# The last two token blocks: one finished and stored first, the other's products in two PSUM banks

## Chip, cores, metric

One core of a Trainium2 chip. The metric is device time in microseconds (us) of one execution; the profile's span, from the first to the last instruction, is about 1.8 us shorter than that time. Engines in the profile: PE is TensorE's matmuls, PEld its weight loads, DVE VectorE, ACT ScalarE, POOL GpSimd, SP SyncE; a q behind a name is that engine's sequencer. Li is line i of the kernel profiled.

## The reference

```python
qn = q / (norm(q, axis=1) + 1e-06);  kn = k / (norm(k, axis=1) + 1e-06)   # B, N, C = 4, 6144, 256
a  = softmax(kn.transpose(0, 2, 1) @ qn / tau)                            # C x C per batch
x  = (v @ a).reshape(B * N, C)                                            # 24576 tokens
h  = maximum(maximum(x @ w1, x @ w2), x @ w3)                             # d_ff = 768
return h @ w_out                                                          # 24576 x 256, float32
```

## The kernel before

The attention matrix is folded into the three weights of each batch, so a chunk of 512 tokens needs 36 products of 512 columns for `h` and 24 of 256 columns for `h @ w_out`. The last chunk is done in two halves of 256 tokens, so that less work is left when the last `h` is there. A token block is 128 tokens, `FC` = 6 pieces of `d_ff`, `P` = 128, `HT` = 2, `CC` = 2.

```python
ps_h = ...tile_pool(name="ps_h", bufs=6, space=PSUM)      # htile: one bank each
ps_x = ...tile_pool(name="ps_x", bufs=2, space=PSUM)      # xtile
...
def last_chunk(gi, aw, pending):
    ...
    def products(ps, t0, i, fcs):
        c0 = i * d_model if t0 == 0 else 0
        for fc in fcs:
            PE.matmul(ps[:, c0:c0 + d_model], lhsT=hts[gi][:, fc, (t0 + i) * P:(t0 + i + 1) * P],
                      rhs=wo_sb[:, fc, :], start=(fc == 0 and c0 == 0), stop=(fc == FC - 1), ...)
    ...                                   # first_half(i): blocks 0 and 1, one copy, one 256 KB store (L440)
    for fc in range(FC):
        h_block(gi, aw, fc, slice(HT, TPC), two_copies=fc in (0, 2, 3))
        if fc >= FC - HT:
            first_half(fc - (FC - HT))
    pss = [htile("o_ps") for _ in range(HT)]
    for fcs in (range(FC - 1), (FC - 1,)):            # the last piece of h is used last
        for i in range(HT):
            products(pss[i], HT, i, fcs)
    ACT.activation(out=o_sb[:, HT, :], in_=pss[0][:, 0:d_model], func=AF.Copy)       # L455
    DVE.tensor_copy(out=o_sb[:, HT + 1, :], in_=pss[1][:, 0:d_model])                # L456
    ACT.dma_start(out=dst[:, HT, :], in_=o_sb[:, HT, :])                             # L457
    SP.dma_start(out=dst[:, HT + 1, :], in_=o_sb[:, HT + 1, :])                      # L458
```

## Time and profile before

| | before |
|---|---|
| device time, median of the first 3 runs | 573.09 us (573.09 to 573.32) |
| span of the profile | 571.7 us |
| last product ends / last store issued | 568.09 / 568.58 |
| last store lands | 570.8 |

TensorE is busy for 97% of the span, and from 560 us on the chain is TensorE's without a gap, so what happens beside it there does not show in the time until it ends. The last 3.65 us, from there to the end, are a chain of a wait, a copy, a store and the closing of the program, and this is the stretch that the change is about. The lines that carry this are in the prediction below. Starts and ends are of the span's clock, so an event of one profile can be set against the same event of another only by its distance from a common point; for the end of this kernel that point is the end of TensorE's last product.

### The profile page before, as it was taken

How to read it: one execution, taken by the hardware profiler on the slowest of the kernel's cores; microseconds unless marked ns; L12 is line 12 of the kernel's file. 1: busy time of each engine (PE TensorE's matmuls, PEld its weight loads, DVE VectorE, ACT ScalarE, POOL GpSimd, SP SyncE). 2: the span in 40 equal slices, each digit the busy share in tenths (PEclk: the TensorE clock that was granted, in tenths of full speed). 3: DMA queues.
4: the chain of work that ended last, by engine and by line, in shares of the span. 5: the costliest groups of instructions: out<-in, count | busy, mean ns of one | idle time of the engine just before them, and what ended most of it. 6: DMA issues, size and time to landing. Idle time of an engine off the chain costs nothing.

```text
span 571.7 us, 9440 instructions
## 1 busy us (share of the span) xinstructions
PE 553.0 (97%) x3343; PEld 329.8 (58%) x3344; DVE 415.7 (73%) x658; ACT 310.4 (54%) x543; POOL 233.6 (41%) x237
## 2 busy tenths in 40 slices
PE   3789999999999999999999999999999999999997
PEld 2665555555755555555575555555575555555566
DVE  0048777777887778777768777777868778778775
ACT  1044567767464576776545467767645444444444
POOL 2441357776460078776560048777750000000000
PEclk9999999999999999999999999999999999999999
DMA  9996999884669268975279339984437333132112
GB/s 142 104 169 101 130 234 144 157 134 104 114 81 177 66 106 160 132 148 111 57 129 151 97 81 141 150 139 94 129 76 164 74 75 111 56 98 69 56 55 76
DMA packets 76960, 65.64 MB, mean 115 GB/s; under 512 B 52464, under 2 KB 62576, under 8 KB 76784
## 3 DMA queue, kind: packets, MB, share of 16 engines
q0 software_dynamic: 19072, 26.48, 38.8%
q1 hardware_dynamic: 57696, 38.41, 24.6%
q8 instruction: 26, 0.43, 0.3%
q14 instruction: 22, 0.18, 0.1%
q10 hardware_dynamic: 144, 0.13, 0.1%
HBM read 78.64 MB, written 25.17 MB: 182 GB/s over the span
## 4 chain that ended last, share of the span: by engine, by line
PE 93%; DMA 5%; POOL 0%; issue 0%; DVE 0%; POOLq 0%
PE h_ps L379 65%; PE o_ps L403 22%; DMA q_sb<-in_q_dram 5%; PE gram L250 3%; PE ew_ps L301 3%; POOL k_sb L99 0%; PE o_ps L428 0%; PE ew_ps L325 0%; PE warm_ps L464 0%; PE vt_ps L362 0%; PE gram L181 0%; DVE o_sb L456 0%; PE rs_ps L289 0%; PE gram L183 0%; PE rs_ps L319 0%
## 5 line engine op out<-in xcount | busy, mean ns | idle before, releaser
L379 PE MATMUL h_ps<-vt_sb,aw_sb 128*128 128x512 bf16 (+1 forms) x1764 | 406.7, 375 | 0.0
L379 PEld LDWEIGHTS <-aw_sb 128*128 128x128 bf16 x1764 | 171.7, 98 | 161.5 <-DVE aw_sb L307 2.5
L384 DVE TENSOR_TENSOR s_mx<-h_ps,s_mx 128x512 bf16<-128x512 f32 (+1 forms) x294 | 199.0, 677 | 81.8 <-ACT s_mx L383 81.5
L383 ACT ACTIVATE s_mx<-h_ps 128x512 bf16<-128x512 f32 (+1 forms) x294 | 172.6, 587 | 122.5 <-PE h_ps L379 121.4
L389 DVE TENSOR_TENSOR ht_sb<-h_ps,s_mx 128x512 bf16<-128x512 f32 (+1 forms) x291 | 199.0, 684 | 30.3
L209 POOL TENSOR_TENSOR acc<-acc,sq 128x768 f32<-128x768 f32 x88 | 144.3, 1650 | 69.3 <-ACT sq L201 53.2
L403 PE MATMUL o_ps<-wo_sb,ht_sb 128*128 128x256 bf16 x1128 | 153.8, 273 | 0.0
L403 PEld LDWEIGHTS <-ht_sb 128*128 128x128 bf16 x1128 | 110.4, 98 | 52.1
L406 ACT ACTIVATE o_sb<-o_ps 128x512 f32<-128x512 f32 x94 | 56.2, 598 | 83.6 <-PE o_ps L403 83.6
L110 POOL DMA_DIRECT2D v_sb<-in_v_dram x48 | 27.8, 583 | 37.3 <-DMA vt_sb<-v_sb 35.0
L201 ACT ACTIVATE sq<-q_sb 128x768 bf16<-128x768 fp8e4 x48 | 40.6, 846 | 0.0
L201 ACT ACTIVATE sq<-k_sb 128x768 bf16<-128x768 fp8e4 x48 | 40.1, 836 | 0.0
L206 POOL CAST acc<-sq 128x768 f32<-128x768 bf16 x6 | 4.9, 822 | 64.9 <-ACT sq L201 64.9
L102 POOL DMA_DIRECT2D q_sb<-in_q_dram x33 | 18.3, 562 | 4.1 <-DMA v_sb<-in_v_dram 3.5
L169 PE MATMUL kk<-k_sb 128*128 128x256 fp8e4 x48 | 7.5, 338 | 12.4 <-DVE k_sb L155 6.3
L99 POOL DMA_DIRECT2D k_sb<-in_k_dram x29 | 16.0, 553 | 3.2 <-DMA v_sb<-in_v_dram 1.3
L250 PE MATMUL gram<-k_sb,q_sb 128*128 128x512 fp8e4 x144 | 16.8, 277 | 0.0
L304 ACT ACTIVATE aw_sb<-ew_ps,rinv 128x384 bf16<-128x384 f32 (+1 forms) x24 | 13.2, 556 | 5.7 <-PE ew_ps L301 4.8
L250 PEld LDWEIGHTS <-q_sb 128*128 128x256 fp8e4 x144 | 15.9, 136 | 0.6
L222 POOL PARTITION_ALL_REDUCE tot<-acc x6 | 10.9, 1859 | 12.1 <-DVE s_mx L384 6.2
L301 PE MATMUL ew_ps<-w_sb,et 128*128 128x384 bf16 (+1 forms) x96 | 15.6, 313 | 0.0
L169 PEld LDWEIGHTS <-k_sb 128*128 128x256 fp8e4 x48 | 6.4, 182 | 13.3 <-DMA k_sb<-in_k_dram 7.1
(66 smaller groups left out, 120.5 us busy)
## 6 DMA issues: line engine op xcount, KB each, us to landing
out_dram<-o_sb SPq DMA_DIRECT2D x41, 512.0 KB, 2.9
v_sb<-in_v_dram POOLq DMA_DIRECT2D x48, 256.0 KB, 4.1
k_sb<-in_k_dram POOLq DMA_DIRECT2D x24, 192.0 KB, 5.7
q_sb<-in_q_dram POOLq DMA_DIRECT2D x24, 192.0 KB, 7.3
out_dram<-o_sb SPq DMA_DIRECT2D x13, 256.0 KB, 2.0
k_sb<-in_k_dram POOLq DMA_DIRECT2D x5, 256.0 KB, 11.2
w_sb<-in_moe_w_dram POOLq DMA_DIRECT2D x9, 128.0 KB, 5.6
kf<-in_k_dram SPq DMA_DIRECT2D x1, 1024.0 KB, 4.8
```

What stands on the lines that cost most here:

```text
L102: POOL.dma_start(out=qk[b][0][:, g0:g0 + w, :], in_=q_r[b][:, g0:g0 + w, :])
L110: POOL.dma_start(out=t, in_=v_r[gi // NCH, gi % NCH])
L201: ACT.activation(out=sq, in_=src, func=AF.Square)
L209: POOL.tensor_tensor(out=acc, in0=acc, in1=sq, op=ALU.add)
L250: PE.matmul(g[:, j * C:(j + 1) * C], lhsT=qt[:, tsl, j * P:(j + 1) * P], rhs=kt[:, tsl, :], start=(tp == 0 and j == 0), stop=(tp == NG // ...
L301: PE.matmul(ew[:, :w], lhsT=et[:, j, ic * P:(ic + 1) * P], rhs=w_sb[m][:, j, fsl], start=(j == 0), stop=(j == CC - 1))
L379: PE.matmul(t.rearrange("p (t n) -> p t n", n=P), lhsT=aw[m][:, ic, fsl], rhs=vt[:, tsl, ic, :], start=(ic == 0), stop=(ic == CC - 1))
L383: ACT.activation(out=s_mx, in_=hp[0], func=AF.Copy)
L384: DVE.tensor_tensor(out=s_mx, in0=hp[1], in1=s_mx, op=ALU.max)
L389: DVE.tensor_tensor(out=ht, in0=last, in1=s_mx, op=ALU.max)
L403: PE.matmul(st["ps"][:, half], lhsT=ht[:, fc, t * P:(t + 1) * P], rhs=wo_sb[:, fc, :], start=(fc == 0), stop=(fc == FC - 1))
L406: ACT.activation(out=st["o"][:, t - 1:t + 1, :].rearrange("p t d -> p (t d)"), in_=st["ps"], func=AF.Copy)
```

## The change

Intent: finish block 2 some products before block 3, so that its copy and store run while TensorE still works, and make the last step short: block 3's 256 columns are accumulated as two halves in two banks, ScalarE and VectorE each copy a half at the same time, and one store takes both. (Blocks are counted 0 to 3 in the last chunk; `block_1` in the code is block 3. The last store also moves from SP to ACT.)

```diff
--- before.py
+++ after.py
@@ -448,14 +448,26 @@
             h_block(gi, aw, fc, slice(HT, TPC), two_copies=fc in (0, 2, 3))
             if fc >= FC - HT:
                 first_half(fc - (FC - HT))
-        pss = [htile("o_ps") for _ in range(HT)]
-        for fcs in (range(FC - 1), (FC - 1,)):
-            for i in range(HT):
-                products(pss[i], HT, i, fcs)
-        ACT.activation(out=o_sb[:, HT, :], in_=pss[0][:, 0:d_model], func=AF.Copy)
-        DVE.tensor_copy(out=o_sb[:, HT + 1, :], in_=pss[1][:, 0:d_model])
-        ACT.dma_start(out=dst[:, HT, :], in_=o_sb[:, HT, :])
-        SP.dma_start(out=dst[:, HT + 1, :], in_=o_sb[:, HT + 1, :])
+
+
+        pa = htile("o_ps")
+        pb = [htile("o_ps") for _ in range(CC)]
+
+        def block_1(fcs):
+            for fc in fcs:
+                for d in range(CC):
+                    PE.matmul(pb[d][:, 0:P], lhsT=hts[gi][:, fc, (HT + 1) * P:(HT + 2) * P],
+                              rhs=wo_sb[:, fc, d * P:(d + 1) * P], start=(fc == 0), stop=(fc == FC - 1))
+
+        products(pa, HT, 0, range(FC - 1))
+        block_1(range(3))
+        products(pa, HT, 0, (FC - 1,))
+        block_1(range(3, FC))
+        DVE.tensor_copy(out=o_sb[:, HT, :], in_=pa[:, 0:d_model])
+        SP.dma_start(out=dst[:, HT, :], in_=o_sb[:, HT, :])
+        ACT.activation(out=o_sb[:, HT + 1, 0:P], in_=pb[0][:, 0:P], func=AF.Copy)
+        DVE.tensor_copy(out=o_sb[:, HT + 1, P:2 * P], in_=pb[1][:, 0:P])
+        ACT.dma_start(out=dst[:, HT + 1, :], in_=o_sb[:, HT + 1, :])
 
 
     ps = gram(0)
```

## The prediction

> **What bounds the kernel now.** I read the page first for the bound of the whole, then the chain that ended last, in order of time, for the final 12 us, then the timeline of the last microsecond of compute, then the sources of the final stores, and last the DMA view of the stretch in which nothing computes any more. The page:
>
> ```profile
> PE 553.0 (97%) x3343; PEld 329.8 (58%) x3344; DVE 415.7 (73%) x658; ACT 310.4 (54%) x543; POOL 233.6 (41%) x237
> ```
>
> TensorE is busy 97% of a span of 571.7 us, at full granted clock in all slices. The change touches nothing before the last 12 matmuls, so only the end matters. The chain, from 560 us on:
>
> ```profile
> 560.67 4.14 PE h_ps L379 x36
> 564.81 0.66 PE o_ps L428 x6
> 565.47 0.66 PE h_ps L379 x6
> 566.12 1.98 PE o_ps L428 x18
> 568.10 0.02 issue
> 568.13 0.42 DVE o_sb L456
> ```
>
> (start, length, what.) TensorE carries the chain without a gap until 568.10; then a copy of 0.42 us; then the view ends, though the span goes on to 571.7. Those 18 products are 6 of the first half's second block and the 12 that the change rearranges; 1.98 us over 18 is 0.110 us each. The timeline of the end:
>
> ```profile
> 566.92 0.42 DVE L389 TENSOR_TENSOR ht_sb<-h_ps,s_mx 128x256 bf16<-128x256 f32 x1
> ...
> 567.49 0.33 SPq L440 DMA_DIRECT2D out_dram<-o_sb  x1
> 568.02 0.39 ACT L455 ACTIVATE o_sb<-o_ps 128x256 f32<-128x256 f32 x1 [0.55 <-PE o_ps L428]
> 568.13 0.42 DVE L456 COPY o_sb<-o_ps 128x256 f32<-128x256 f32 x1 [0.78 <-PE o_ps L428]
> 568.43 0.41 ACTq L457 DMA_DIRECT2D out_dram<-o_sb  x1
> 568.58 0.33 SPq L458 DMA_DIRECT2D out_dram<-o_sb  x1
> ```
>
> The last ht is ready at 567.34; the two blocks' accumulations end one matmul apart (copies start at 568.02 and 568.13), so both 128 KB stores are issued nearly together, at 568.43 and 568.58. Their times to landing, each from its source line's view (first L457 on ACT's queue, then L458 on SP's):
>
> ```profile
> DMA to landing us min/median/max: 1.9/1.9/1.9
> DMA to landing us min/median/max: 2.2/2.2/2.2
> ```
>
> The landings are thus at 568.43 + 1.9 = 570.3 and 568.58 + 2.2 = 570.8, and the end is 0.9 us after the later one. The DMA view of 569.2 to 571.8 (40 slices of 0.065 us) says why the later issue takes longer:
>
> ```profile
> DMA  0048999999998500004000000000000000000000
> ...
> q1 hardware_dynamic: 144, 0.13, 14.5%
> q10 hardware_dynamic: 144, 0.13, 14.4%
> ```
>
> Both stores' data, 0.13 MB each, move in one unbroken stretch from slice 2 to slice 14, 569.33 to about 570.2. Looking at the same stretch in shorter windows, from 569.65 on all 144 packets of q1 (SP) are there but only 41 of q10 (ACT): ACT's data goes first and SP's starts when it is nearly through. One store alone needs about 0.4 us of that stretch, so SP's store waits some 0.25 to 0.3 us on the other. That is where 2.2 against 1.9 us comes from. The bound of the end is therefore: TensorE to 568.1, copy 0.42, issue, data queued behind the other block's data, landing, 0.9 us of closing.
>
> **What the Trainium skill says.** "TensorE: Matmul & The Clock Gate", section "Back-to-back issue gap", gives about 81 ns for each pair of weight load and matmul at N=128 in a sustained stream, and 134 cycles (56 ns at 2.4 GHz) for the isolated gap. This matters because 6 products of 256 columns become 12 of 128. The trace of before has eight N=128 bf16 products, each with its own weight load; in the chain near 36 us they read
>
> ```profile
> 35.86 0.45 PE vt_ps L362 x8
> ```
>
> which is 56 ns each. They are transposes, so the match isn't perfect, but the trace sides with 56 and I use it. "VectorE: DVE Perf Modes", section "The TRN2 errata — SBUF-src ops pay a fixed extra latency per instruction", gives PSUM to SBUF 120 + FD cycles for VectorE and 172 + FD for ScalarE, so halving a copy doesn't halve its time. The slopes in the trace agree: ScalarE 382 ns at 256 columns and 596 at 512 (0.836 ns a column), VectorE 418 to 425 and 688 (1.03 ns a column). "DMA: Bandwidth & Descriptors", section "Issuing engines are not separate DMA queues", says that transfers issued by different engines run on the same 16 DMA engines and interleave; the packets above agree that they share, though here one went almost wholly ahead of the other. "PSUM — Partial Sum Buffer", section "PSUM bank collisions raise a hardware error", is why the halves need two banks: ScalarE and VectorE may not read one bank at once. No run so far shows that.
>
> **The change part by part.**
>
> *TensorE.* Removed: 6 products of N=256 for the last block, 6 x 0.110 = 0.66 us. Added: 12 of N=128, 12 x 0.056 = 0.67 us. The sum is zero within 0.02 us; there are 6 more weight loads, which should hide. The order is new. The 12 products of before start at 568.10 - 12 x 0.110 = 566.78 in the chain's modelled ends. Now: pa's first five to 567.33; six halves to 567.67; pa's last to 567.78; six halves to 568.11. pa's last product needs the ht of 567.34 and is ready to issue only a third of a microsecond after that by ends, about 0.1 us when counted from its weight load, so no wait. The third PSUM buffer rotates onto one that VectorE's combination before the last read, finished about 566.5, while its first matmul is due after 567.1: no wait either.
>
> *The completed block ahead.* pa is complete at 567.78, so VectorE copies it 567.81 to 568.23 (0.425 us, gap of 0.03 as before) and SP issues its store at about 568.26, which is 0.17 us ahead of the first final issue of before. All of it lies beside TensorE's last halves.
>
> *The last block.* ScalarE copies 128 columns from 568.09 (its half ends one matmul earlier) in 386 - 128 x 0.836 = 279 ns, to 568.37. VectorE could start at 568.15, with a length of 425 - 128 x 1.03 = 292 ns. Its previous copy ends at 568.23; adjacent VectorE instructions in the trace start up to 0.08 us before the profiled end of the one before (566.06 + 0.42 against 566.40), so it starts between 568.15 and 568.23 and ends between 568.44 and 568.52. ACT issues about 0.03 later, at 568.47 to 568.55, in place of 568.58: a gain of 0.03 to 0.11, middle 0.07 us.
>
> *The landing.* SP's pa store starts its data about 0.8 to 0.9 us after issue (as ACT's did: 568.43 to 569.33), so 569.1 to about 569.45. The last store's data is due at 568.5 + 0.9 = 569.4, when the other is all but done. Its landing should take 1.9 to 1.95 us, in place of 2.24 (568.58 to 570.82, with the closing chain's semaphore wait): a gain of about 0.30 us.
>
> Sum: TensorE 0.00 (+0.02), issue -0.07, landing -0.30: about -0.36 us. Predicted time 573.09 - 0.36 = 572.73 us.
>
> **Rivals.** (a) The N=128 products cost the skill's 81 ns: 12 x 25 = 0.30 us more on TensorE, of which all moves the last copies. Time about 573.03. For: twice as many weight loads with half the stream to hide them, each 98 ns in the trace. Against: the 56 ns of the eight transposes, and four N=1 products in 0.08 us of the chain. (b) VectorE becomes the bound: its pa copy holds up the last half, and the store now waits for two engines. Worth 0.08 us at worst as computed, 0.1 more if the cross-engine wait is slow: 572.8 to 572.9. (c) The two stores' data still overlap, for they are only 0.2 to 0.3 us apart and each takes 0.35: then the landing stays at 2.1 to 2.2 and the time is 572.9 to 573.0. For: SP's 256 KB store of 567.49 is also still moving until about 569.0, just before pa's data. Against: it ends by then, and before, the same 256 KB had no visible effect. (d) More than thought: if the last store finds idle DMA engines and both copies overlap fully, 572.6. Nothing gets near 2% (11.5 us): from TensorE's end to the end of the span there are only 3.6 us.
>
> **Range and chances.** The runs of before spread over 0.23 us, as large as the effect. Rivals (a) to (c) each have perhaps one chance in six and all push towards 573.0; 572.45 at the low side allows for (d) and the spread, 573.10 at the high side for a gain lost entirely. Faster or slower by 2% would need a failure that this place in the program can't make.
>
> **What would show it.** After: the first combination-free product group should still begin near 566.1 and TensorE end within 0.05 us of 568.1 (later by 0.3: rival a). VectorE's 256-column copy should start near 567.8, before TensorE's end. The two short copies should be about 0.28 and 0.29 us and start within 0.15 us of each other. ACT's store should be issued at 568.5 and land in 1.9 to 2.0 us; if issue is earlier but landing 2.2, it was (c). The closing 0.9 us after the last landing should not change. The prediction is wrong if the last landing isn't 0.25 to 0.45 us before the old 570.8, or if TensorE waits inside the rearranged products.

## The result, and the profile after

| | before | after |
|---|---|---|
| device time, median of 6 runs | 573.11 us (573.01 to 573.97) | 572.90 us (572.74 to 573.17) |
| span of the profile | 571.741 | 571.391 |
| last product ends | 568.087 | 567.931 |
| last store issued | 568.578 | 568.347 |
| SP's wait for its landing ends | 570.822 | 570.473 |

The ratio is 0.9994, with a 95% interval of 0.9981 to 1.0007: no change that these runs can tell from none, and in the predicted range. (A ratio is the mean time of one kernel's fast runs over that of the other's of the same rounds, so it is not quite the ratio of the medians.) What the change may have done is therefore read from the two profiles, one of each kernel, and from nothing else.

The chain that ended last, in the kernel after, from 560 us on (start, length, what):

```profile
560.50 4.14 PE h_ps L379 x36
564.64 0.66 PE o_ps L428 x6
565.30 0.66 PE h_ps L379 x6
565.95 1.20 PE o_ps L428 x11
567.15 0.34 PE o_ps L459 x6
567.49 0.12 PE o_ps L428
567.61 0.02 issue
567.63 0.42 DVE o_sb L466
568.06 0.20 DVE o_sb L469
```

The whole line-up is 0.17 us earlier than before (560.50 against 560.67, with the same 4.14 us). The rest of the view is the changed end: six half products (L459) take 0.34 us, 56 ns each, and block 2's last product (L428) comes between the halves, without a gap. The chain leaves TensorE at 567.61 and goes through VectorE: its 256-column copy of block 2, then its half of block 3. The other six halves, which end at 567.93, are beside that copy. The view puts VectorE's second copy down to its first; but that copy starts 0.045 us after the halves end, so it is TensorE's end that it had to wait for (see rival (b) below).

The 0.17 us are not the change's. The same view of both kernels near 34 us, first before, then after:

```profile
34.00 0.32 PE gram L181
...
37.90 0.33 PE h_ps L379
```

```profile
33.88 0.31 PE gram L181
...
37.74 0.33 PE h_ps L379
```

The first batch's Gram products, which wait for q as it is loaded, are 0.12 us earlier in the profile of after, and the first `h` product 0.16 us. Both kernels run the same instructions there. Of the 0.350 us between the two spans, 0.17 were there before the changed part began; 0.18 are left for it.

The timeline of the end, after:

```profile
567.63 0.42 DVE L466 COPY o_sb<-o_ps 128x256 f32<-128x256 f32 x1 [0.46 <-PE o_ps L428]
567.91 0.28 ACT L468 ACTIVATE o_sb<-o_ps 128x128 f32<-128x128 f32 x1 [0.62 <-PE o_ps L459]
567.98 0.28 DVE L469 COPY o_sb<-o_ps 128x128 f32<-128x128 f32 x1
568.09 0.33 SPq L467 DMA_DIRECT2D out_dram<-o_sb  x1
568.35 0.37 ACTq L470 DMA_DIRECT2D out_dram<-o_sb  x1
```

VectorE copies block 2 before TensorE is done, its half of block 3 starts 0.06 us behind ScalarE's, and SP issues block 2's store (L467) 0.26 us ahead of the last one (L470). VectorE's half starts at 567.98, though its previous copy is shown to last until 568.06: the two overlap by 0.08 us.

The times from issue to landing, by source line, after: block 2's store (L467) in the first fence, the last one (L470) in the second, the 256 KB store of the first half (L440, the same line in both kernels) in the third:

```profile
DMA to landing us min/median/max: 1.9/1.9/1.9
```

```profile
DMA to landing us min/median/max: 2.1/2.1/2.1
```

```profile
DMA to landing us min/median/max: 2.0/2.0/2.0
```

The last store gained 0.1 us against the 2.2 of before, not 0.3. It takes longer than a store of twice the size. The DMA view of 568.8 to 571.4 in the kernel after, again 40 slices of 0.065 us:

```profile
DMA  3059999999999516000000000000000000000000
...
q1 hardware_dynamic: 161, 0.14, 15.9%
q10 hardware_dynamic: 144, 0.13, 14.5%
q14 instruction: 1, 0.01, 1.5%
```

The two stores' data still follow one another without a pause. Packet by packet, the trace has block 2's data (q1) from 568.94 to 569.44 and the last store's (q10) from 569.30 to 569.78: an overlap of 0.14 us. Before, the overlap was 0.14 us too (569.69 to 569.83); what differs is how long the second store had waited by then: its first packet came 1.11 us behind its issue, and now 0.95. In both kernels that packet starts 0.006 us after the first of the sixteen 4-byte packets that end the first store's data (569.682 and 569.688 before, 569.290 and 569.296 after). So the second store seems to take its turn behind the first still, with far less to wait.

From the end of the last product on, the end divides as follows (us; the times of packets and waits are of the trace's records, and each term is a difference of two of them; the fourth, from the last packet to the landing, is called the receipt below):

| | before (store on SP) | after (store on ACT) | gain |
|---|---|---|---|
| last product's end to last issue | 0.491 | 0.416 | 0.075 |
| issue to the store's first data packet | 1.110 | 0.949 | 0.161 |
| first data packet to the end of the last packet | 0.493 | 0.494 | 0.00 |
| last packet to the end of SP's wait for the landing | 0.641 | 0.683 | -0.04 |
| from there to the end of the span | 0.919 | 0.918 | 0.00 |
| sum | 3.654 | 3.460 | 0.194 |

TensorE gives 0.015 of this back (0.171 earlier at the start of the last stretch, 0.156 earlier at its end), which leaves 0.18.

The second row mixes two things. SP's stores that weren't held up began their data 0.83 to 0.86 us after issue, ACT's of before 0.914. An estimate from these (ACT's 0.914 is a single store): SP's last store had waited some 0.25 to 0.28 us behind the other one, ACT's waits 0.035 at most, and some 0.06 to 0.08 of the difference is given back because ACT starts later than SP. No run has the last store of the new order on SP.

### The profile page after: what moved, and what is told of

Its sections match the earlier page's. It is cut to its first block, busy times and chain, and to the rows that moved or that the text cites. A ratio compares the mean times of both kernels' runs of the same rounds, so it can differ in the third digit from the quotient of the medians.

```text
span 571.4 us, 9454 instructions
## 1 busy us (share of the span) xinstructions
PE 552.0 (97%) x3349; PEld 328.5 (57%) x3350; DVE 415.9 (73%) x659; ACT 310.0 (54%) x543; POOL 233.3 (41%) x237
## 4 chain that ended last, share of the span: by engine, by line
PE 94%; DMA 2%; issue 2%; POOL 1%; DVE 0%; POOLq 0%
PE h_ps L379 65%; PE o_ps L403 22%; PE gram L250 3%; PE ew_ps L301 3%; DMA q_sb<-in_q_dram 2%; POOL q_sb L102 0%; POOL k_sb L99 0%; PE o_ps L428 0%; PE gram L181 0%; PE ew_ps L325 0%; PE warm_ps L476 0%; PE gram L183 0%; PE vt_ps L362 0%; DVE o_sb L466 0%; PE o_ps L459 0%
## 5 line engine op out<-in xcount | busy, mean ns | idle before, releaser
L384 DVE TENSOR_TENSOR s_mx<-h_ps,s_mx 128x512 bf16<-128x512 f32 (+1 forms) x294 | 198.9, 677 | 82.2 <-ACT s_mx L383 81.9
L389 DVE TENSOR_TENSOR ht_sb<-h_ps,s_mx 128x512 bf16<-128x512 f32 (+1 forms) x291 | 199.0, 684 | 30.3
```

Of the source, the lines that this page charges most:

```text
L384: DVE.tensor_tensor(out=s_mx, in0=hp[1], in1=s_mx, op=ALU.max)
L389: DVE.tensor_tensor(out=ht, in0=last, in1=s_mx, op=ALU.max)
```

## The experiments

None gave a result, so nothing here is shown by experiment. Four kernels were made first, the changed one again and three that are each one step away from it.

**again**: the changed kernel, unaltered, to see how much of its end repeats.

> The changed kernel unaltered, to see what of its tail repeats. In its first profile the last product ended at 567.93, the last store was issued at 568.35 (0.42 later) and took 2.13 to land, against 2.24 before and 1.96 hoped for; its last data packet left at 569.79, so the receipt took 0.68 us, where the stores that were not last took 0.53 to 0.57. If the slow receipt is chance, this profile shows 1.95 to 2.0 from issue to landing; if it belongs to the kernel, 2.1 to 2.15 again. Last product's end to last issue should be 0.40 to 0.43 in either case. Time: 572.8 to 573.0, ratio 0.9994 to 0.9998 with an interval that includes 1.

(Its "0.53 to 0.57" for stores that were not last fits the first of each 128 KB pair alone; the 256 KB stores had 0.34 to 0.41.)

**order_only**: block 2 is still ahead, but block 3 is whole.

```diff
-        pb = [htile("o_ps") for _ in range(CC)]
+        pb = htile("o_ps")
-                for d in range(CC):
-                    PE.matmul(pb[d][:, 0:P], ...)    # cut short here
+                products(pb, HT, 1, (fc,))
-        ACT.activation(out=o_sb[:, HT + 1, 0:P], in_=pb[0][:, 0:P], func=AF.Copy)
-        DVE.tensor_copy(out=o_sb[:, HT + 1, P:2 * P], in_=pb[1][:, 0:P])
+        ACT.activation(out=o_sb[:, HT + 1, :], in_=pb[:, 0:d_model], func=AF.Copy)
```

> The first block still completed and stored ahead, but the last block's products whole (256 columns, one bank) and copied by ScalarE alone. Theory (the gain is the earlier first store, which takes its data out of the last store's way): last product's end to last issue 0.45 (0.04 wait, 0.386 copy, 0.03), so 0.03 later than with halves, issue to landing as in the changed kernel, 2.0 to 2.15, and the time within 0.1 us of the changed kernel's. Rival (the halved copies in two banks bring the gain): the time goes back to the 573.1 of before.

**halves_only**: the halves in two banks, but block 2 finished late.

```diff
-        block_1(range(3))
+        block_1(range(FC - 1))
         products(pa, HT, 0, (FC - 1,))
-        block_1(range(3, FC))
+        block_1((FC - 1,))
```

> The last block in halves of two banks, copied by both engines for one store, but the first block's last product only just before the last block's last two, as in the kernel before. Theory (the gain is the store ahead): VectorE's 256-column copy of the first block starts about 0.1 before TensorE's end and holds up its half copy, last product's end to last issue 0.55 to 0.65 in place of 0.42, the first store only 0.2 to 0.25 ahead, so issue to landing 2.1 to 2.25; end of last product to last landing 2.75 to 2.85, as before (2.73) or worse, time 573.0 to 573.2. Rival (the halves bring the gain): last issue 0.42 after the end as in the changed kernel, time 572.9.

**no_pa_store**: without block 2's store, a wrong result on purpose. REFUSED.

```diff
-        SP.dma_start(out=dst[:, HT, :], in_=o_sb[:, HT, :])
```

> Wrong result on purpose: the changed kernel without the store of the completed block, so that the last store has the DMA engines to itself. If the first store's data or receipts delay the last one, issue to landing falls from 2.13 to 1.9 to 1.98 and the time by 0.15 to 0.2 us below the changed kernel's. If the last store's receipt is slow whatever lies next to it, issue to landing stays at 2.05 to 2.1 (0.04 less for the data that starts unhindered).

Last, at 13:36, came one kernel that was to replay nine forms of the end side by side, each four times, so that the terms of the table above would have had repeats. No chip ran it either.

**replays**: no result.

```diff
+    for _ in range(4):
+        for tail in (tail_before, tail_after, tail_order, tail_halves, tail_alone, tail_nolead, tail_joint,
+                     tail_onsp, tail_small):
+            tail()        # 30 filler products, the first half's blocks, copy and store, then the form
+    # each tail writes to its own slice of a scratch tensor, so that no store waits for another's landing
```

> Nine forms of the end replayed in one kernel, four times each in turn, behind filler products, into scratch memory (ordinary fp8 Gram products in place of paired ones; its time, 850 to 950 us, says nothing). Read: P, end of last product to last issue; L, issue to landing. So far: before P 0.49, L 2.23; changed P 0.42, L 2.11. Theory: the gain is the store ahead. Rival: the halved copies bring it. Also: is the slow last receipt chance, a neighbour's doing, or a thing of the program's end. BEFORE 0.49, 2.2 to 2.25. AFTER 0.40 to 0.43; L 1.95 to 2.0 if the slow receipt is chance or the program's end, 2.1 if the neighbour's. ORDER (store ahead, last block whole in one bank, ScalarE's copy): P 0.45, L as AFTER; by the rival its sum is BEFORE's. HALVES (halves, first block completed only just before the end): P 0.55 to 0.65, L 2.1 to 2.25, sum no better than BEFORE; by the rival AFTER's sum. ALONE (AFTER without the first block's store): L 1.9 to 1.95, 0.05 below AFTER if only data overlaps, 0.15 to 0.2 if receipts suffer. NOLEAD (AFTER without the 256 KB store): as AFTER within 0.05. JOINT (one 256 KB store of both blocks at the end): L 2.1 to 2.25. ONSP (AFTER, last store issued by SP): L 0.05 to 0.1 shorter. SMALL (first block and left half of the last in one store ahead, the 64 KB right half last): P 0.35, L 0.1 to 0.2 shorter. Repeats should agree within 0.1 in L; where they spread more than forms differ, nothing is told apart.

So the questions in these texts stand open: which part of the change brought the 0.18 us, whether the slow last landing repeats, and what makes it slow.

## Why the prediction was right, and where it was not

The time, 572.90, was forecast as 572.73 within 572.45 to 573.10: inside the range and the class; the forecast was 0.17 too low. That says little: the range also holds the 573.09 of before, so no gain at all would have been inside it. By its steps:

- **TensorE unchanged** (forecast +0.02): 0.015 later. The twelve half products ran at 56 ns with a weight load each, as the eight transposes of before had said. Rival (a), the 81 ns that the Trainium skill's "TensorE: Matmul & The Clock Gate", section "Back-to-back issue gap", gives for a sustained stream, didn't come about in these two runs of six: it would have put TensorE's end 0.30 later.
- **No wait for `h` or for a bank**: right. The chain shows no gap inside the products. Block 2's last weight load started at 567.27; the `h` piece that it needs was done at 566.75 + 0.425 = 567.175, so 0.1 us was to spare.
- **Copies** (forecast 279 ns on ScalarE and 292 on VectorE, VectorE's start 0 to 0.08 behind): measured 277 and 284, VectorE's start 0.06 behind ScalarE's. Rival (b), VectorE's earlier copy in the way, came to nothing: its half started 0.045 after TensorE's end, about the 0.039 that the same copy took to start before. Scaling by the slope of measured sizes was right within 3% (VectorE's 1.03 ns a column mixes L389 at 256 columns with L384 at 512; like for like it is 1.04 to 1.05, and the forecast 290 to 292); a proportional guess (half of 386 and 425) would have been 0.07 to 0.08 us too short.
- **Last issue** (forecast 0.03 to 0.11 earlier, middle 0.07): 0.075.
- **Landing** (forecast 0.30 shorter, "1.9 to 1.95 us, in place of 2.24"): 2.126, so 0.118 shorter. This is the term that was mis-sized, and it is nearly all of the difference between the forecast 0.36 and the 0.18 found. The mechanism, that the second store's data waited on the first's, was there: its data started 0.161 sooner after issue. But I took the whole 1.96 us of before's first store as what a store takes once it is not held up, and that store differed from the one it stood for in two ways. It began its data 0.914 after issue, and the last store now took 0.949, which is 0.035. And its last packet was 0.552 ahead of the wait's end, where for the last store it was 0.683, which is 0.131. Together with 0.004 of data they make 0.170, the distance from 1.956 to 2.126; the rest of the shortfall of 0.18 is that I rounded 2.244 - 1.956 = 0.288 up to 0.30.

Rival (c), data that still overlap, has the right numbers (a landing of 2.1 to 2.2, 572.9 to 573.0 us), for the wrong reason: the overlap is 0.14 us, as before, but the delay that can be put down to it is at most the 0.035. The prediction also had one store's data as 0.35 to 0.4 us; each of the four took 0.49 to 0.50 from its first packet to its last, so an overlap had to be expected. What ate most of the expected gain was the time after the data, which no step of the prediction had looked at by itself. It could have: before, too, the second store took 0.09 longer from its last packet than the first one (0.641 against 0.552), a part of "2.2 against 1.9" that the prediction put down to queued data alone.

The prediction's own signs divide in the same way. Taken from TensorE's end, the copies and the last issue came as it said (issue 0.42 us behind), and the closing 0.92 did not change; the store's landing in "1.9 to 2.0" did not come. Its test of being wrong, the last landing 0.25 to 0.45 us before the old 570.8, is passed with 0.35, but by luck: 0.16 of that is TensorE's earlier end, which comes from the earlier start. From TensorE's end the landing is 0.19 earlier, outside that test.

Why the last store's receipt is long is open. In both traces the 256 KB stores from 530 us on have their last packet 0.34 to 0.41 us ahead of their landing (7 in each; an eighth, whose 16 parts land spread over 0.9 to 1.4 us, 0.47). In the pair of 128 KB stores, the first has 0.54 before and 0.53 after, the second 0.63 and 0.67. Another store's data close behind is not enough: in the kernel after, L440's last packet ended at 568.943, block 2's data began at 568.944 and ran past L440's landing at 569.298, and L440 had 0.355 all the same. What is left: the pair's stores have packets of 1 KB instead of 2 KB; the second is the program's last; and in both traces an 8 KB instruction fetch (q14) was under way in the second one's receipt and ended within 0.06 us of the landing (570.809 and 570.806 before, 570.404 and 570.456 after). Against the last: a longer fetch (q8, from 541.5) lay over the landing of the 256 KB store of 539.9 in both traces, and that store had 0.34. No run separates these. The Trainium skill's "DMA: Bandwidth & Descriptors", section "Anatomy of one DMA — SWDGE (gpsimd) path", says that the fixed part of about 2 us is mostly the write's receipt from the target memory. In this trace the part after the last packet is 0.34 to 0.67 of 1.9 to 2.2 us, less than the 0.83 to 0.95 from issue to first data of the stores that weren't held up; these were issued by SP and ACT, and the page's figure is for GpSimd's path, so the two are not the same measurement.

That the measured time fell by 0.21 (medians) does not contradict 0.18, but the runs of one kernel spread over 0.43 to 0.96 us, and the start alone moved by 0.17 between two profiles. The prediction called the spread "as large as the effect"; the times neither confirm nor refute the sum.

## What to carry to other kernels

At the end of a program that one engine bounds, draw the chain behind that engine's last instruction and size each link: wait, copy, issue, start of data, data, receipt, closing. Here some 2.9 of 3.65 us (start of data 0.9, data 0.5, receipt 0.6, closing 0.9) are links that this change did not shorten; what it moved was the issue and the queueing of data. A store's time to landing did not go by its size here (2.0 us for the 256 KB of L440, 1.9 to 2.2 for 128 KB): split it into start of data, data and receipt before taking one store's number for another's.

## What the Trainium skill lacked or had wrong

- "TensorE: Matmul & The Clock Gate", "Back-to-back issue gap": its 81 ns for a sustained stream of weight load and matmul at N=128 was not met. Twelve bf16 products with a load each, and eight transposes, ran 56 ns apart, the page's figure for the isolated gap. These came in runs of six and eight; no run here has a longer stream.
- "VectorE: DVE Perf Modes", "The TRN2 errata — SBUF-src ops pay a fixed extra latency per instruction": from PSUM, 128 columns of fp32 took 284 ns on VectorE and 277 on ScalarE in the profile; its 120 + FD and 172 + FD cycles (with its divisor Accel at 1) are 258 and 250 ns at the clocks it gives.
- "DMA: Bandwidth & Descriptors", "Anatomy of one DMA — SWDGE (gpsimd) path": the split is of GpSimd's path alone, and the page has no time from the last packet to the landing for stores issued by SP or ACT. In these traces it was 0.34 to 0.67 us, the longest for the second of two 128 KB stores close together. Issue to first data, for which another section of the page has a first-byte figure, was 0.83 to 0.86 us on SP and 0.91 to 0.95 on ACT.
